# Loading and spreading V of the last batch eight half-slots sooner, and a new order for the first batches, in a windowed attention + MLP kernel

## The chip, the cores and the metric

The kernel runs on one NeuronCore of a Trainium2 chip. Its time is the device time of one execution in microseconds (us). Engines are named as in the profile: PE (TensorE matmul), PEld (its weight loads), DVE (VectorE), ACT (ScalarE), POOL (GpSimd), SP (SyncE). SP only issues DMAs; ACT and POOL issue some as well.

## The reference, cut to what matters

```python
q, k, v: [8 batches, 8 heads, 576 positions, 64]        # float32
scores = q @ k.T / sqrt(64); kept where 0 <= query - key < 64
attn   = softmax(scores);     o = attn @ v               # [8, 8, 576, 64]
x = o.transpose(0, 2, 1, 3).reshape(4608, 512)
h = x @ w_in                                             # [512, 2048]
g = h - tanh(h)
out = g @ w_out                                          # [2048, 512], float32
```

## The kernel before, in words

**Attention.** A batch b has four pairs of heads; a pair is one unit `g = 4*b + pr`, 32 units in all. A unit is worked as follows. Q and K arrive as rows (`load`, `load_all`), are cast to a bfloat16 row tile (`cast`; tiles `qb` and `kb`, three buffers each), and are turned by PE transposes into PSUM, from where ACT or DVE copy them to `qT` and `kT` (`tr`; two buffers each). `scores` makes three groups of three score blocks, with an exponential on ACT behind each group; units below 8 add the mask with a second matmul (`hide`), later units multiply it on DVE (`masking`). `pv` multiplies by V in three groups of three, and `norm` divides on DVE (a reciprocal and two products). Finished heads are turned into `xT`, by PE transposes (`x_tr`) for the first two batches and by DMA transposes (`x_dma`) for the others.

**V.** V of a batch is loaded into one tile `vall` (one buffer: the next load waits until all four casts have read it). Four casts (`cast_v`, one for each pair) bring it to `vb` (one buffer). Nine small DMAs (`keys_v`, 65 KB each) move it to the upper half of `vw[b % 2]`, and a shift (`shift_v`, one DMA of 520 KB on SP, or two DVE copies for the first two batches) fills the lower half. A cast of the next batch into `vb` waits until all nine of these small DMAs have landed. `pv` needs the shift.

**The MLP** is cut into 9 chunks of 512 tokens. For a chunk, `hp_mm` (L304, 16 times) makes h, ACT takes the tanh, `g_sub` (L314, DVE) makes g, and `yp_mm` (L324) multiplies g of 16 slots earlier by w_out; `y_out` copies the result on ACT and stores it from SP.

**The order** is written out by hand. The kernel counts half-slots h; an even h issues `hp_mm`, an odd one `yp_mm`, and then whatever `items[h]` holds. For batches 3 to 7 the items stand in a loop of formulas: for unit g, `a = 8*g - 48 - (0, 2 or 4)` and for its batch `s = 32*b - (0, 2 or 4)`; for the last batch a = 172, 180, 188, 196 and s = 220. The last batch (b = 7) does not use PE transposes for Q and K: it writes the cast rows to DRAM (`bounce`: `qd`, `kd`) and reads them back with a DMA transpose (`tr_dma`), all on SP:

```python
at(a - 12, bounce, g, "q")      # a - 11 for k
at(a - 6, tr_dma, g, "q")       # a - 5 for k
at(s - 54 + j // 2, keys_v, b, j)
at(s - 47, shift_v, b, 0, NJ - 1)
```

`pace(h)` lets POOL wait for the slot's g before it issues a load. The first three batches are in `PLAN`, a table of short codes. The number is a unit (or a batch, or a batch and a part) in base 36, and a last letter names the engine (a ACT, v DVE, p POOL, s SP). The codes of interest are: `q`/`r` load Q/K of a pair; `Q`/`K`/`V` load a whole batch; `a`/`b` cast Q/K; `d` cast V; `k` move keys (`keys_v`); `z` shift; `E`/`F` turn Q/K (`tr`); `R` scores; `P` pv and norm; `X` x_tr; `w`/`o` weights of the two matmuls; `n` the mask; `m`/`i` constants. Key -1 of the table is everything that is issued ahead of the first `hp_mm`. Each engine runs its own instructions in the order of issue, so an order in this table is an order in each engine's queue.

Of the kernel before, what the change touches and what calls it, by code (L numbers as in the profile page):

```python
# [15 lines left out]
def kernel(  # L16
# [12 lines left out]
    NJ = S // 64  # L29
# [307 lines left out]
    def at(h, *fn):  # L337
        items.setdefault(h, []).append(fn)
# [14 lines left out]
    def play(script):  # L353
        for step in script.split():
# [50 lines left out]

    PLAN = {
        -1: """
            r2a q0s v02 v03 v00 v01 a0v r0s d00a d01v d02a m i r1p q3p q1a d03p b0a k01s a1v
            k08s k00s b1p k03p n k02s F0a E0av R01 R02 q2p E1av k07p V1 k06a a3p k04p b2v K1 a2a
            R00 F1v k05s r3a E2aa F2a Q1 w0 R10 z0v d12p R22 d13p R12 P0 R11 E3aa R20 P1 d10p  # L410
            b3a d11p k12s k13p R21 k16p a7p w1 F3a b4a P2 a4p R30 R31 X000v Q2 R32 P3 b7a X001a
            k10s K2 b5p a6p F4a k18s w2 X010v k11s k17s b6p a5p b9p V2 k15a X011v E4vv""",
        0: "b8p",
        10: "R42 F5v k14s E5aa",
        12: "a8v R41 o2 o1 a9p d20p z1v",
        15: "R50 o3 R40 E6av F6v d21p R51 R52 E7aa P4 d22p R62 F7a R61 bAa o0 d23p P5 k25s R60",
        16: "E8aa k23p aAp R70",
        20: "R72 k20s X100v k27s X101a P6",
        23: "F8a R71 F9a k21p k22p aBp R80 P7 E9av k26s bBp k24p R82",
        24: "R81 X111v k28s X110a R91",  # L420
        31: "R90 z2s EAav M8",
        32: "R92",
        35: "FAa",
        36: "RA1 M9",
        41: "P9 RA0 FBa",
        45: "P8 RA2 EBav",
        50: "MA RB2 RB0 PA RB1",
        56: "MB PB",
        58: "Y2",
    }  # L430
    for h, script in PLAN.items():
        at(h, play, script)
# [5 lines left out]
    for g in range(3 * NP, B * NP):  # L438
        b, pr = divmod(g, NP)
        a = 8 * g - 48 - (0, 2, 4)[min(b - 3, 2)]  # L440
        s = 32 * b - (0, 2, 4)[min(b - 3, 2)]
        at(s - 72 + 5 * pr, cast_v, b, pr)
        if b < 7:
            at(a - 7, cast, g, "q")
            at(a, tr, g, "q", 3, nc.scalar, nc.vector)
        else:
            at(a - 14, cast_q, g)
            at(a - 12, bounce, g, "q")
            at(a - 6, tr_dma, g, "q")
        if b < 7:  # L450
            at(a - 5, cast, g, "k")
            at(a + 2, tr, g, "k", 3, nc.scalar)
        else:
            at(a - 13, cast, g, "k")
            at(a - 11, bounce, g, "k")
            at(a - 5, tr_dma, g, "k")
        for i in range(3):
            at(a + 5 + 2 * i, scores, g, i, 4)
        at(a + 11, masking, g)
        for i in range(3):  # L460
            at(a + 13 + i, pv, g, i)
        at(a + 15, norm, g)
        if pr == NP - 1:
            at(a + 16, x_dma, b)
        for j in range(NJ):
            if pr == 0:
                at(s - 54 + j // 2, keys_v, b, j)
        if pr == 0:
            if b < 4:
                at(s - 78, load_v_all, b)  # L470
                at(s - 64, load_all, b, "q")
                at(s - 63, load_all, b, "k")
            else:
                hq, hk = s - (60 if b < 7 else 68), s - (64 if b < 7 else 72)
                for h, f in (s - 78, (load_v_all, b)), (hq, (load_all, b, "q")), (hk, (load_all, b, "k")):
                    at(h, pace, h)
                    at(h, *f)
            at(s - 47, shift_v, b, 0, NJ - 1)

    LAG = 16  # L480
    for h in range(min(items), 2 * (16 * NC + LAG) + 2):
        n = h // 2
        c, m = divmod(n, M)
# [41 lines left out]
```

The softmax here doesn't subtract the row's maximum and nothing guards it: scores larger than these inputs give would overflow.

## Time and profile before

| | |
|---|---|
| median of 4 runs | 353.82 us (352.15 to 355.24) |
| profiled execution: its own time / its span | 352.77 us / 351.1 us |
| PE busy | 315.2 us (90%) |
| DVE, ACT, POOL busy | 198.1, 192.8, 112.0 us |
| first PE instruction | 13.87 us after the span's start |
| first `hp_mm` | 38.90 us |
| last PE work ends, last instruction ends | 347.1 us, 351.1 us |

PE is busy 315.2 us out of 351.1 us, so the idle 35.9 us are what another order could shorten with the same work. They are read by stage: each stretch's length minus its PE busy time. In stretches where PE shows no idle time, what another engine does costs nothing.

### The profile page before, as it was taken

The numbers are of one execution on the slowest core, as the hardware profiler recorded it, in microseconds if no ns is written. First come the engines' busy times: TensorE is split into PE (matmuls) and PEld (weight loads), VectorE is DVE, ScalarE is ACT, GpSimd is POOL, SyncE is SP. The second block draws the span as 40 slices with busy tenths as digits, with TensorE's granted clock in tenths as the row PEclk, the third lists the DMA queues.
The fourth block names the chain that finished last, engine by engine and source line by source line (L and its number), as shares of the span: only waits on it lengthen the run. The fifth ranks groups of instructions, "written<-read, shape, count | busy, mean of one in ns | idle before, by whom it ended". The sixth has DMA issues, their size and how long they took to land.

```text
span 351.1 us, 5740 instructions
## 1 busy us (share of the span) xinstructions
PE 315.2 (90%) x2173; PEld 179.1 (51%) x2173; DVE 198.1 (56%) x314; ACT 192.8 (55%) x347; POOL 112.0 (32%) x160
## 2 busy tenths in 40 slices
PE   0277788899899999999999999997999999999995
PEld 0266456555555555555555555553555444444442
DVE  1336776866776666666767667664656333344400
ACT  1467479865556665666566666553554444444411
POOL 7829633925337424522452262610000000000000
PEclk9999999999999999999999999999999999999999
DMA  8699999969777786877595798559821400010021
GB/s 174 124 157 192 163 191 171 175 132 182 158 157 121 128 124 151 132 146 135 131 132 128 147 158 142 111 141 221 189 74 40 120 32 30 32 59 30 30 90 61
DMA packets 54436, 43.98 MB, mean 125 GB/s; under 512 B 25144, under 2 KB 48248, under 8 KB 54024
## 3 DMA queue, kind: packets, MB, share of 16 engines
q0 software_dynamic: 20512, 18.22, 35.9%
q1 hardware_dynamic: 33128, 24.37, 27.1%
q10 hardware_dynamic: 768, 1.02, 1.0%
q8 instruction: 17, 0.28, 0.3%
q14 instruction: 11, 0.09, 0.1%
HBM read 36.70 MB, written 11.21 MB: 136 GB/s over the span
## 4 chain that ended last, share of the span: by engine, by line
PE 70%; DMA 15%; POOL 5%; DVE 5%; ACT 2%; issue 1%; SPq 0%; ACTq 0%; POOLq 0%; DVEq 0%
PE ps L324 32%; PE ps L304 29%; DMA vw<-vb 5%; DMA vall<-in_v_dram 4%; PE ps L261 4%; DMA kall<-in_k_dram 4%; PE ps L247 3%; PE ps L234 2%; DVE xs L272 2%; DMA vw<-vw 1%; DVE gT L314 1%; POOL vb L84 1%; POOL qb L84 1%; POOL vw L161 1%; DMA kt<-kd 1%
## 5 line engine op out<-in xcount | busy, mean ns | idle before, releaser
L314 DVE TENSOR_TENSOR gT<-ps,th 128x512 bf16<-128x512 f32 x144 | 99.3, 691 | 94.5 <-ACT th L308 92.1
L304 PE MATMUL ps<-xT,wi 128*128 128x512 bf16 x576 | 147.3, 379 | 1.7 <-DVE gT L314 1.7
L324 PE MATMUL ps<-w_out_sb,gT 128*128 128x512 bf16 x576 | 145.2, 379 | 0.2 <-ACT ysb L329 0.2
L308 ACT ACTIVATE th<-ps 128x512 f32<-128x512 f32 x144 | 85.9, 598 | 79.4 <-PE ps L304 79.1
L304 PEld LDWEIGHTS <-wi 128*128 128x128 bf16 x576 | 61.0, 113 | 47.5 <-issue 3.1
L324 PEld LDWEIGHTS <-gT 128*128 128x128 bf16 x576 | 54.1, 98 | 55.8 <-issue 0.5
L251 ACT ACTIVATE pt<-ps 128x384 bf16<-128x384 f32 x96 | 46.9, 490 | 44.5 <-PE ps L247 37.6
L272 DVE TENSOR_TENSOR xs<-ps,rc 64x576 bf16<-64x576 f32 x64 | 48.3, 755 | 1.5
L84 POOL COPY vb<-vall 72x1024 bf16<-72x1024 bf16 x29 | 30.7, 1074 | 52.3 <-DMA vall<-in_v_dram 38.8
L247 PE MATMUL ps<-qt,kt 128*128 128x128 bf16 x288 | 36.8, 227 | 7.7 <-ACT pt L251 3.8
L261 PE MATMUL ps<-vw,pt 128*128 128x130 bf16 x288 | 29.7, 226 | 4.4 <-DMA vw<-vw 1.5
L261 PEld LDWEIGHTS <-pt 128*128 128x128 bf16 x288 | 22.6, 101 | 20.9 <-issue 3.9
L247 PEld LDWEIGHTS <-kt 128*128 128x128 bf16 x288 | 24.5, 102 | 11.4 <-ACT kt L82 1.9
L329 ACT ACTIVATE ysb<-ps 128x512 f32<-128x512 f32 x36 | 21.5, 597 | 16.0 <-PE ps L324 16.0
L84 DVE COPY qt<-ps 64x576 bf16<-64x576 bf16 x24 | 18.2, 759 | 18.7 <-ACT qt L82 18.7
L84 POOL COPY kb<-kall 96x768 bf16<-96x768 bf16 x26 | 21.6, 832 | 13.4 <-DMA kall<-in_k_dram 13.1
L84 POOL COPY qb<-qall 96x768 bf16<-96x768 bf16 x24 | 20.0, 832 | 16.2 <-PE ps L304 6.8
L82 ACT ACTIVATE qt<-ps 64x576 bf16<-64x576 bf16 x32 | 20.4, 636 | 1.2 <-PE ps L234 0.9
L82 ACT ACTIVATE kt<-ps 128x576 bf16<-128x576 bf16 x25 | 16.2, 648 | 4.4 <-PE ps L234 4.2
L255 DVE TENSOR_TENSOR pt<-pt,ps 128x1152 bf16<-128x1152 bf16 x24 | 17.9, 744 | 0.0
L234 PE MATMUL ps<-ident,kb 96*128 96x96 bf16 x168 | 12.6, 214 | 2.0 <-ACT xT L82 0.9
L234 PEld LDWEIGHTS <-kb 96*128 96x128 bf16 x168 | 10.5, 103 | 6.9 <-issue 2.4
(52 smaller groups left out, 123.8 us busy)
## 6 DMA issues: line engine op xcount, KB each, us to landing
out_dram<-ysb SPq DMA_DIRECT2D x36, 256.0 KB
vall<-in_v_dram POOLq DMA_DIRECT2D x7, 576.0 KB, 9.6
kall<-in_k_dram POOLq DMA_DIRECT2D x7, 576.0 KB, 9.2
qall<-in_q_dram POOLq DMA_DIRECT2D x7, 576.0 KB, 8.2
vw<-vb SPq DMA_DIRECT2D x61, 65.0 KB
vw<-vw SPq DMA_DIRECT2D x6, 520.0 KB
w_out_sb<-in_moe_w_out_dram POOLq DMA_DIRECT2D x4, 512.0 KB, 8.6
qd<-qz SPq DMA_DIRECT2D x4, 288.0 KB
```

Of the source, the lines that this page charges most:

```text
L82: nc.scalar.activation(o, i, ACT.Copy)
L84: eng.tensor_copy(o, i)
L234: nc.tensor.transpose(tp[:, e, :], src[:, e, :], ident[:P, :P])
L247: nc.tensor.matmul(sp[:, i, :], kT[g % NR][:, 64 * j:64 * j + 128], qT[g % NR][:, :, 64 * j:64 * j + 64], start=True, stop=g >= 2 * NP)
L251: nc.scalar.activation(PT[g % NPT][:, 3 * grp:3 * grp + 3, :], sp, ACT.Exp, scale=scale)
L261: nc.tensor.matmul(ps[:, 5 + grp, 130 * i:130 * i + 130], PT[g % NPT][:, j, :], vw[b % 2][:, j, 2 * pr:2 * pr + 2, :], start=True, stop=True)
L272: nc.vector.tensor_tensor(xo[r, :, :, pr, :], ov[r, :, :, h, 0:D], rc[r].to_broadcast([64, 3, 3, 64]), ALU.mult)
L304: nc.tensor.matmul(hp, w_in_tile(ki, m), chunk_tile(c)[:, :, ki % 2, 64 * (ki // 2):64 * (ki // 2) + 64], start=(ki == 0), stop=(ki == 3))
L308: nc.scalar.activation(th, hp, ACT.Tanh)
L314: nc.vector.tensor_tensor(gT[c][:, m, :], hp, th, ALU.subtract)
L324: nc.tensor.matmul(yp, gT[c][:, m, s * 128:(s + 1) * 128], w_out_sb[:, m, :], start=(m == 0), stop=(m == M - 1))
L329: nc.scalar.activation(ysb, ps[:, yp_bank(c, s), :], ACT.Copy)
```

## The change

Two parts. **V of the last batch:** a new `sv = s - 8` for b = 7 (212 in place of 220) replaces s in the half-slots of its load and pacing (h = 134, was 142), its four casts (140, 145, 150, 155; were 148, 153, 158, 163), its nine key moves (158 to 162; were 166 to 170) and its shift (165; was 173). Q and K of that batch stay where they were, and so do all bounces and DMA transposes. **The first batches:** the table `PLAN` is written anew. The PE work is the same (4348 PE instructions in both programs); the order and the engine of some copies, key moves and first loads differ.

```diff
-        at(s - 72 + 5 * pr, cast_v, b, pr)
+        sv = s if b < 7 else s - 8
+        at(sv - 72 + 5 * pr, cast_v, b, pr)
...
-                at(s - 54 + j // 2, keys_v, b, j)
+                at(sv - 54 + j // 2, keys_v, b, j)
...
-                for h, f in (s - 78, (load_v_all, b)), (hq, (load_all, b, "q")), (hk, (load_all, b, "k")):
+                for h, f in (sv - 78, (load_v_all, b)), (hq, (load_all, b, "q")), (hk, (load_all, b, "k")):
...
-            at(s - 47, shift_v, b, 0, NJ - 1)
+            at(sv - 47, shift_v, b, 0, NJ - 1)
```

```diff
     PLAN = {
         -1: """
-            r2a q0s v02 v03 v00 v01 a0v r0s d00a d01v d02a m i r1p q3p q1a d03p b0a k01s a1v
-            k08s k00s b1p k03p n k02s F0a E0av R01 R02 q2p E1av k07p V1 k06a a3p k04p b2v K1 a2a
-            R00 F1v k05s r3a E2aa F2a Q1 w0 R10 z0v d12p R22 d13p R12 P0 R11 E3aa R20 P1 d10p
-            b3a d11p k12s k13p R21 k16p a7p w1 F3a b4a P2 a4p R30 R31 X000v Q2 R32 P3 b7a X001a
-            k10s K2 b5p a6p F4a k18s w2 X010v k11s k17s b6p a5p b9p V2 k15a X011v E4vv""",
-        0: "b8p",
-        10: "R42 F5v k14s E5aa",
-        12: "a8v R41 o2 o1 a9p d20p z1v",
-        15: "R50 o3 R40 E6av F6v d21p R51 R52 E7aa P4 d22p R62 F7a R61 bAa o0 d23p P5 k25s R60",
-        16: "E8aa k23p aAp R70",
-        20: "R72 k20s X100v k27s X101a P6",
-        23: "F8a R71 F9a k21p k22p aBp R80 P7 E9av k26s bBp k24p R82",
-        24: "R81 X111v k28s X110a R91",
-        31: "R90 z2s EAav M8",
+            v00 v03 v02 q0s v01 r1p d00a r0s i q1s m d02a d03p b0a b1p r2s a0v d01v k08s F0v
+            k00s E0av k02a k01s q3p k03a a1a E1av q2p n V1 a3p b2p k06a k05s k07p R02 R01 k04p K1
+            r3a F1v a2a d11p R00 R12 Q1 z0v E2av d12a R10 P0 R11 F2a E3va R22 d10v R21 w0 P1
+            d13v b3p w1 R20 F3a P2 a7p k16s b4p k18s R30 X000v k17s R32 k10s a4p K2 k13s a5p R31
+            k14s k11s k12p P3 b7p a6p X001a Q2 k15s b5a w2 b6p X010v X011v b8p E4aa""",
+        0: "F4a",
+        10: "b9p R42",
+        12: "V2 F5v o2 R41 o0 z1v",
+        15: """
+            E5aa o1 R40 a8v R51 d20p F6v E6av a9p R50 d22p R52 d23p E7aa P4 o3 d21p R62 F7a R61
+            k26p P5 k27s bAa R60""",
+        16: "E8aa aAp R70",
+        20: "R72 X101a X100v P6",
+        23: "F8a k25s k20s k28s R71 F9a k23s P7 R82 k22s k24s k21p z2s aBp R81 E9av R80",
+        24: "X111v R91",
+        25: "X110v",
+        31: "bBp FAa R90",
...
```

## The prediction

> **What bounds the kernel now.** First the busy rows by slice, on the page:
>
> ```profile
> PE   0277788899899999999999999997999999999995
> DMA  8699999969777786877595798559821400010021
> ```
>
> PE is the bound from slice 8 (about 70 us) on; ahead of it PE is starved while the DMA engines are full. Idle by stretch, from the windows of busy time: 13.87 us before the first PE instruction, 10.98 from there to 60 us, 2.99 from 60 to 100, 4.0 from 100 to 300, of which 2.56 lie between 230 and 250, and 4 at the end (the last copy and store). Only these 35.9 us can move. The waits of PE from 225 to 260 us name the 2.56:
>
> ```profile
> PE ps L247 <- DMA kt<-kd: 1.4, 1, 1.4
> PE ps L261 <- DMA vw<-vw: 1.2, 1, 1.2
> ```
>
> SP's own timeline shows why those two DMAs come late (start, length with the wait in it):
>
> ```profile
> 229.91 2.38 SPq L161 DMA_DIRECT2D vw<-vb  x2
> ...
> 232.83 0.87 SPq L161 DMA_DIRECT2D vw<-vb  x1
> 235.16 0.52 SPq L169 DMA_DIRECT2D vw<-vw  x1
> 235.79 2.76 SPq L137 DMA_TRANSPOSE qt<-qd  x1
> 238.59 1.26 SPq L140 DMA_TRANSPOSE kt<-kd  x1
> ```
>
> The shift (L169) waits for the last key move, and the transposes of unit 29 stand behind it. The front's binding chain is in the chain of waits, in order of time:
>
> ```profile
> 35.73 13.55 DMA kall<-in_k_dram
> ...
> 50.20 9.57 DMA vall<-in_v_dram
> ...
> 70.08 6.73 DMA vw<-vb
> ...
> 76.99 4.22 DMA vw<-vw
> 81.21 0.05 issue
> 81.26 0.63 PE ps L261 x8
> ```
>
> K of batch 2 lands, POOL casts a piece, V of batch 2 (V2) is issued, its casts and key moves follow, then the shift; unit 9's pv waits 0.31 us for it. So at 81.26 PE and the V2 chain are nearly level: PE gaining time before that point keeps it only if the V2 chain gains too.
>
> **Part 1, V of the last batch (h = 134 to 165).** No instruction is added or removed; nine key moves, the shift, four casts and a load move ahead.
>
> *On SP.* The key moves go ahead of the bounces and transposes of units 28 and 29. Four are issued from about 209.6 (the last cast follows unit 26's cast), at some 0.65 each. The bounces of unit 28 wait, as before, for Q of this batch, which lands at 217.0 (`qz` cast 216.98): 218.3 and 219.6. The last key move is issued at 221.3, about 2 us to land (before, 232.83 + 0.87 to the shift at 235.16), shift at 223.4, landing 4.2 later (76.99's row) at 227.6; pv of unit 28 reads it at 238.46. Transposes of unit 28 follow at 223.9 and 225.2 (before 221.01, 223.78), landing near 228.5; scores of unit 28 want them at 230.71: 2 us of cover. Unit 29: transposes issued by 233.2 in place of 239.85; wanted at 240.1. Both stalls go: **-2.56**.
>
> *What is late next:* unit 30. Its transposes ended at 247.90 on SP and its scores began at 249.53 with a gap of only 0.09; they stood behind two xT transposes (241.51, 3.08). That group is issued some 2.5 us sooner too, as far as PE is. I charge 0.1.
>
> *On POOL.* The new load stands after unit 24's cast (188.27), so at 189.1. The first V cast now stands ahead of unit 25's Q cast (before at 189.81) and waits for the load. PE turns unit 25 at 200.69. Landing times of V loads here: 7.9 (195.7's) to 11.1 (15.0's), median 9.6. With 9.1 (160.5's, the one whose place in its batch is like this one's): 198.2, + 1.05 V cast + 0.84 Q cast = 200.1, in time; at 11.1 a stall of 1.4. The overlap with batch 6's key moves (to 191.9) and shift (193.64) speaks for 9 to 10. I charge 0.2. Part 1: **-2.3**, between -2.6 and -1.0.
>
> [...] The row first: at 230 to 240 us the DMA share is 0.70, not full, and the delay is SP's in-order wait between the last key move (232.83) and the shift (235.16), not bytes. [...]
>
> **Part 2, the new table.** Same PE work; I walk the new order with durations of the rows (a cast 0.83 or 1.05, DMA issue 0.65 to 0.85, six transposes 0.66 and 0.42, score triple 0.8 cold and 0.5 warm; matmuls start 0.107 apart until 33.16 and 0.055 after, and I keep that moment).
>
> - *Start.* PE waited for the mask (POOL, 13.87). Now K and Q of unit 0 stand ahead of the mask: V casts on ACT from about 7.9, kb at 11.0, PE at 11.1: -2.8 at the first instruction. It hides nothing yet: pv of unit 0 needs key moves behind V of batch 1 in POOL's DMA ring.
> - *pv of unit 0.* V1 is issued at 13.5 (was 15.02) and took 11.1; with the key moves behind it landing at 24.5 (was 26.36), pv ends at 25.9 (was 27.78): -1.9.
> - *First `hp_mm`.* Less was done ahead of pv (R22 and F2 move behind it), DVE has 0.76 + 2 x 0.43 more between the norms, and each pv waits for a norm (0.22 + 1.52): P1 29.0, P2 32.0, P3 34.6, `hp_mm` at 38.3 (was 38.90): -0.6. Q1 and w0 are issued at 25.6 and 26.4 (were 17.98 and 18.76) because POOL's V1 cast now stands ahead of them; in the old order POOL stood still behind them instead. They land near 33 and 35.5: w0 has some 3 us of cover.
> - *h = 0 to 15.* F4 is now behind the first `hp_mm` and E5 in h = 15 with both copies on ACT (1.29) in front of the exponentials on which the next scores wait: R40 48.5, R51 50.9, F6 51.2, R50 51.9, R52 53.1, P4 53.7, P5 56.2, ninth `hp_mm` 57.1 (was 56.50): **+0.6**. The lead is gone.
> - *V2 chain.* Its load now stands behind unit 9's K cast, whose buffer F6 frees: cast 51.5, V2 at 52.4 (was 50.20). Then: landing 8.8 (between 7.9 and 9.57, as w2 is further on), 61.2; casts, one Q cast and weight load to V3's issue 6.95 (was 6.81), 68.2; the one key move behind V3 in the ring lands with it, 9.5 + 0.4, 78.1 (was 76.81); shift 0.2 + 4.2; pv of unit 9 at **82.5** (was 81.26). PE arrives at 81.3 to 81.4, so the chain decides: **+1.25**. Later gates have slack: batch 3's shift is wanted only at 105.7, nine us after it landed.
>
> [...]
>
> **Sum.** -2.3 + 1.25 = -1.0 us: 352.77 - 1.0 = 351.8 for the profiled execution, which lies 1.05 below the median; from 353.82, **352.8 us**.
>
> **Rivals.**
>
> 1. *The gate doesn't bind* (0.25). V2 and V3 land in 7.9 us, as one load did, and the lead at pv of unit 0 (-1.9) survives h = 15. Against it: ACT's two copies there. Then part 2 gives -2 and the whole -4.3: 349.5.
> 2. *V2 comes later, slower* (0.17). Q2 and w2 (2.1 MB read) now wait for E4's buffer and go out at 39.3 and 40.1 (were 34.93 and 38.04). w2 took 17.0 us, and V2 landed 4.7 behind it. If the ring is emptied late, w2 at 60 (the ninth `hp_mm` wants it at 57.1) and V2 at 64.7: gate 86.0, +4.7 - 2.3: 356.2. It decides once V2 lands after 62.3, where part 1 is used up. For it: at 20 to 60 us the DMA share is about 1; against it: fewer bytes are left in front of w2.
> 3. *Part 1 doesn't do what it says* (0.08): unit 25's cast or unit 30's transposes stall by what unit 29 gains. Then only +1.25 stays: 355.1.
>
> The forecast has 0.50. **Range** 349.0 to 357.0: the first reaches to rival 1, the second past rival 2. About 1% (3.5 us) is what a measurement here can tell from no change. Faster by more: most of rival 1, 0.22; slower: much of rival 2 and tails, 0.18; within 1%: 0.60.
>
> **What would show it.** First PE work near 11 us; pv of unit 0 ending near 26; first `hp_mm` at 38.3; ninth near 57; V2 issued near 52.4; pv of unit 9 waiting for `vw<-vw` by about 1 us, near 82.5; no PE wait for `vw<-vw` or `kt<-kd` at 225 to 260; at most a few tenths on unit 25's transpose near 202. A V2 landing before 60 or after 63, or a ninth `hp_mm` off by over 2 us, makes it wrong.

## The result, and the profile after

The changed kernel takes 355.77 us, the median of 32 runs (353.84 to 359.10), against 353.87 us of the kernel before beside it; the ratio is 1.0075 (95% interval 1.0056 to 1.0095). So it is **slower by 0.75%**, a small change, but clear of the noise. Its profiled execution took 355.78 us with a span of 354.1 us, 3.0 us more than the span before. PE is busy as long as before (315.1 us). The forecast was a gain of 1.0 us.

The rows by slice, of the changed kernel:

```profile
PE   0258777898899999999999989999999999999995
...
PEclk9999899999999999999999999999999999999999
DMA  8699996976986959786597689488701410010011
```

Read against the rows before, slices counted from 0: PE's 7 at slice 27 has become a 9, which is part 1's gain. The 8 at slice 23 is new. In the front, slices 2 to 6, three of PE's digits are lower, one is equal and one is higher. PEclk has an 8 in slice 4, where the page of before has 9 throughout. (The 9s ahead of it do not mean full speed, see below at the clock.)

**The tail.** From 225 to 260 us the list of PE's waits has no row at all: both stalls, 1.4 and 1.2 us, are gone. PE is busy for all of these 35.00 us; before it was for 32.44. SP's timeline of that stretch, changed kernel (start, length with the wait in it):

```profile
228.41 0.52 SPq L169 DMA_DIRECT2D vw<-vw  x1
229.04 2.77 SPq L137 DMA_TRANSPOSE qt<-qd  x1
231.85 1.25 SPq L140 DMA_TRANSPOSE kt<-kd  x1
...
236.78 1.23 SPq L137 DMA_TRANSPOSE qt<-qd  x1
238.10 1.21 SPq L140 DMA_TRANSPOSE kt<-kd  x1
```

The shift goes out at 228.41 in place of 235.16, although PE is six microseconds later than before by then. It now stands in front of the transposes of unit 28 (229.04, 231.85), and those of unit 29 (236.78, 238.10) no longer stand behind it. But from 110 to 225 us a wait is new (PE's waits, changed kernel):

```profile
PE ps L234 <- POOL qb L84: 1.4, 1, 1.4
```

That is unit 25: its Q cast stands on POOL behind the first V cast, and that one waits for the load.

**The front.** PE's timeline (start, length, and in brackets the idle time before it and its releaser), of the kernel before:

```profile
27.19 0.59 PE L261 MATMUL ps<-vw,pt 128*128 128x130 bf16 x4 [0.52 <-DVE vw L167]
28.21 0.69 PE L234 MATMUL ps<-ident,qb 96*128 96x96 bf16 x6
29.65 1.14 PE L261 MATMUL ps<-vw,pt 128*128 128x130 bf16 x9
...
37.00 0.41 PE L234 MATMUL ps<-ident,kb 96*128 96x96 bf16 x6 [0.85 <-ACT xT L82]
```

And of the changed kernel:

```profile
27.08 0.59 PE L261 MATMUL ps<-vw,pt 128*128 128x130 bf16 x4 [0.52 <-DVE vw L167]
...
30.79 1.18 PE L261 MATMUL ps<-vw,pt 128*128 128x130 bf16 x9
...
40.27 1.91 PE L304 MATMUL ps<-xT,wi 128*128 128x512 bf16 x4
41.97 0.69 PE L234 MATMUL ps<-ident,kb 96*128 96x96 bf16 x6
```

pv of unit 0 ends at 27.67, as late as before (27.78). pv of unit 1 starts 1.14 us later than before (29.65), the first `hp_mm` 1.37 later (38.90), the ninth at 60.00 (56.50). The four matmuls at 40.27 take 1.70 us to the next instruction; four of them take 0.86 later (81.04 to 81.90). The busy windows show why (columns: PE, PEld, DVE, ACT, POOL, granted clock, DMA share, GB/s):

```profile
39.00:40.00 1.00, 0.77 (x12) 0.64 (x13) 0.65 (x2) 0.00 (x0) 0.69 (x1) 0.79 0.95 184
40.00:41.00 1.00, 1.00 (x8) 0.56 (x7) 0.26 (x2) 0.45 (x1) 0.04 (x1) 0.50 1.03 132
...
43.00:44.00 1.00, 1.00 (x6) 0.48 (x5) 0.54 (x1) 0.61 (x2) 1.00 (x2) 1.00 1.03 207
```

The granted clock is at half (0.50) from 39.6 to 43.0, in the middle of the first matmuls of the MLP.

pv of unit 0 waits for the last key moves of batch 0. POOL's timeline of the changed kernel shows why these are late:

```profile
11.81 0.82 POOL L84 COPY kb<-kall 96x768 bf16<-96x768 bf16 x1 [2.02 <-DMA kall<-in_k_dram]
...
15.21 0.84 POOL L151 DMA_DIRECT2D vall<-in_v_dram  x1 [0.39 <-issue]
...
18.78 1.18 POOL L161 DMA_DIRECT2D vw<-vb  x2
```

POOL waits for K of unit 1, issues V of batch 1 (V1) at 15.21 (before 15.02), and reaches the two key moves behind it only at 18.78.

**The V2 chain.** POOL's timeline, changed kernel: the load of V2 stands behind a K cast that waits for PE (and so does an earlier K cast, at 50.20).

```profile
54.55 0.82 POOL L84 COPY kb<-kall 96x768 bf16<-96x768 bf16 x1 [3.52 <-PE ps L234]
55.32 0.86 POOL L151 DMA_DIRECT2D vall<-in_v_dram  x1
```

It goes out at 55.32 (before 50.20). The chain of waits ends that way at 86.2, where unit 9's pv has waited 1.5 us:

```profile
73.41 7.92 DMA vw<-vb
81.58 4.62 DMA vw<-vw
```

So by marks the changed kernel is late by 1.4 at the first `hp_mm`, by 3.5 at the ninth and by 5.0 at pv of unit 9 (81.26 before). Then follow 4.7 ahead of unit 25, 6.3 behind it and 3.3 behind the tail, by the starts of the same matmuls in both; the spans differ by 3.0.

### The profile page after: what moved, and what is told of

It reads as the page before. It is cut to its first block, busy times and chain, and to the rows that moved or that the text cites. A ratio compares the mean times of both kernels' runs of the same rounds, so it can differ in the third digit from the quotient of the medians.

```text
span 354.1 us, 5753 instructions
## 1 busy us (share of the span) xinstructions
PE 315.1 (89%) x2173; PEld 179.6 (51%) x2173; DVE 198.8 (56%) x315; ACT 193.0 (55%) x346; POOL 108.7 (31%) x156
## 3 DMA queue, kind: packets, MB, share of 16 engines
q1 hardware_dynamic: 33760, 25.16, 27.3%
## 4 chain that ended last, share of the span: by engine, by line
PE 74%; DMA 11%; DVE 5%; ACT 4%; POOL 2%; issue 2%; SPq 1%; POOLq 0%; ACTq 0%; DVEq 0%
PE ps L324 31%; PE ps L304 30%; DMA vw<-vb 6%; PE ps L261 5%; PE ps L247 4%; PE ps L234 3%; DVE xs L272 2%; DMA kall<-in_k_dram 2%; DVE gT L314 1%; DMA vw<-vw 1%; DMA qall<-in_q_dram 1%; ACT qt L82 1%; ACT pt L251 1%; ACT th L308 1%; POOL vall L146 1%
## 5 line engine op out<-in xcount | busy, mean ns | idle before, releaser
L251 ACT ACTIVATE pt<-ps 128x384 bf16<-128x384 f32 x96 | 46.8, 490 | 37.8 <-PE ps L247 33.1
L84 POOL COPY vb<-vall 72x1024 bf16<-72x1024 bf16 x26 | 27.8, 1077 | 57.6 <-DMA vall<-in_v_dram 42.4
L329 ACT ACTIVATE ysb<-ps 128x512 f32<-128x512 f32 x36 | 21.5, 596 | 16.0 <-PE ps L324 15.7
L84 POOL COPY qb<-qall 96x768 bf16<-96x768 bf16 x24 | 19.9, 830 | 25.8 <-DMA qall<-in_q_dram 24.6
L84 DVE COPY qt<-ps 64x576 bf16<-64x576 bf16 x23 | 17.5, 760 | 17.7 <-ACT qt L82 17.6
L234 PE MATMUL ps<-ident,kb 96*128 96x96 bf16 x168 | 12.9, 218 | 12.8 <-ACT kb L82 12.1
```

Source lines behind the costliest of these rows:

```text
L84: eng.tensor_copy(o, i)
L234: nc.tensor.transpose(tp[:, e, :], src[:, e, :], ident[:P, :P])
L251: nc.scalar.activation(PT[g % NPT][:, 3 * grp:3 * grp + 3, :], sp, ACT.Exp, scale=scale)
L329: nc.scalar.activation(ysb, ps[:, yp_bank(c, s), :], ACT.Copy)
```

## The experiments

Ratios are against the kernel before, run beside each; spans are those of the profiled execution. The theories: **A**, the new table costs the time (through waits that the runs below name one by one); **B**, V sooner costs it; **T**, PE's clock in the front is a part of its own.

### Which part

Part 1 alone, in the kernel before:

```diff
+        sv = s if b < 7 else s - 8       # s -> sv in load, casts, key moves, shift
```

> The kernel before with part 1 alone (the table of the first batches stays old). Theory A (the table costs the time): both stalls of 225 to 260 us go (-2.56), unit 25's transposes wait about 1.4 us for a Q cast that stands behind the first V cast (+1.4): span 350.0, about 1.1 us below before. Rival B (V sooner costs it): the load of V among batch 6's key moves takes back more than it gives: span 351 to 353, no gain or a loss.

Measured: ratio 0.9960 (0.9925 to 0.9994), span 350.2. No PE wait from 225 to 260 us. POOL's timeline of it at unit 25:

```profile
189.22 0.82 POOL L151 DMA_DIRECT2D vall<-in_v_dram  x1
...
200.98 1.05 POOL L84 COPY vb<-vall 72x1024 bf16<-72x1024 bf16 x1 [10.11 <-DMA vall<-in_v_dram]
201.97 0.82 POOL L84 COPY qb<-qall 96x768 bf16<-96x768 bf16 x1
```

The load was cast 11.8 us after its issue, and PE waited 2.0 us for the Q cast behind it.

The new table alone:

```diff
-        sv = s if b < 7 else s - 8
+        sv = s
```

> The changed kernel with the V of the last batch at its old half-slots (the new table alone). Theory A: ninth hp_mm near 60.0 (before 56.50), pv of unit 9 near 86.2, both stalls of 225 to 260 us back: span 355.2, 4 us above before. Rival B: the new table costs at most the forecast 1.25, span near 352.4, and the rest comes from part 1.

Measured: ratio 1.0115 (1.0069 to 1.0161), span 356.1. The PE waits from 225 us on are those of before again, to the tenth, and unit 25 does not wait. The two ratios multiply to 1.0075, the ratio of both parts together. Theory A holds and B falls: **part 1 gives 0.4%, the new table costs 1.15%**.

### Part 1 without its own stall

```diff
-        at(sv - 72 + 5 * pr, cast_v, b, pr)                       # v_qfirst
+        at(sv - (72 if b < 7 else 70) + 5 * pr, cast_v, b, pr)
```
```diff
-        sv = s if b < 7 else s - 8                                # v_four
+        sv = s if b < 7 else s - 4
```

> Part 1 alone with its four V casts two half-slots later (142, 147, 152, 157), so that unit 25's Q cast stands ahead of the first V cast on POOL; load, key moves and shift as in part 1. Theory A (the order on POOL makes the stall): unit 25's wait of 1.4 us goes, the gain of 2.56 stays: span 348.6, 2.5 us below before. Rival C (the landing of V is late in itself and the key moves of batch 6 share its DMA engines): the Q cast goes but another wait comes, span 350 or more.

> Part 1 alone by four half-slots in place of eight (load 138, casts 144 to 159, key moves from 162, shift 169). Theory A: the first V cast comes behind unit 25's Q cast, so no wait there; key moves and shift stand ahead of the transposes of unit 29 by enough: both stalls gone or nearly, span 348.6 to 349.2. Rival C: unit 28's transposes, issued at the same half-slots as the last key moves (166 and 167), wait for those, and a stall of 1 us or more stays: span 350 or more.

Measured: 0.9942 (0.9907 to 0.9976), span 348.4; and 0.9943 (0.9906 to 0.9981), span 347.3. In both the wait at unit 25 is gone, though V lands no sooner (the first cast of it is at 201.29 and 202.07). POOL of v_qfirst:

```profile
191.84 0.82 POOL L84 COPY qb<-qall 96x768 bf16<-96x768 bf16 x1
201.29 1.05 POOL L84 COPY vb<-vall 72x1024 bf16<-72x1024 bf16 x1 [8.63 <-DMA vall<-in_v_dram]
```

The Q cast runs nine microseconds ahead of the V cast in place of behind it. So the stall came from the order on POOL and not from bytes (rival C falls). With four half-slots only 0.2 us of wait is left in the tail, so the transposes of unit 28 do not suffer. Neither ratio can be told from that of part 1 alone; the waits in the traces are what separates them.

### Which stretch of the new table

The old table ahead of the first `hp_mm`, the new one behind it, with part 1:

```diff
     PLAN = {
-        -1: """ (new) """, 0: "F4a", 10: "b9p R42", 12: "V2 F5v o2 R41 o0 z1v",
+        -1: """ (old, with b9p V2 and F4a) """, 0: "b8p", 10: "R42 k14s", 12: "F5v o2 R41 o0 z1v",
         15: """ (new)
```

> Part 1 with the old table ahead of the first hp_mm and the new table from half-slot 0 on (V2 stays where the old table had it, and so do unit 8's and 9's K casts and F4). Theory B (the loss is made ahead of the first hp_mm): first hp_mm 38.9, ninth 57.2 (E5's copies in half-slot 15 cost 0.7), span 350.2 to 351, ratio near 0.998. Rival I (the new order after slot 0 costs most): ninth 58.5 or later, span 352.5 or more.

Measured: 0.9945 (0.9914 to 0.9975), span 350.5; first `hp_mm` 38.22, ninth 57.90. This is as fast as part 1 alone. So **the whole loss is made by what the new table issues ahead of the first `hp_mm`, or has pushed from there into the first slots** (V2, unit 9's K cast, F4). Theory B of this run holds; the order from slot 15 on costs nothing that can be measured.

### Undoing the named waits

Three edits of the changed kernel, one by one and together:

```diff
-  ... R12 Q1 z0v E2av d12a R10 P0 R11 F2a E3va R22 d10v R21 w0 P1       # a_hoist
+  ... R12 Q1 E2aa R10 R11 F2a R22 R21 E3aa z0v P0 d12a d10v w0 P1
```
```diff
-  b6p X010v X011v b8p E4aa""", 0: "F4a", 10: "b9p R42", ... 15: "E5aa o1 R40   # a_f4e5
+  b6p F4a X010v X011v b8p E4aa""", 10: "b9p R42 E5aa", ... 15: "o1 R40
```
```diff
-  b8p E4aa""", ... 12: "V2 F5v                                          # a_v2
+  V2 b8p E4aa""", ... 12: "F5v
```

> The changed kernel, with the scores of units 1 and 2 and the turning of units 2 and 3 put back in front of pv of unit 0 (ACT does both halves of E2 and E3; ACT's cast of V behind them). Theory A1 (2.8 us of cold PE work stand between pv of unit 0 and pv of unit 1 where PE used to idle for V): pv of unit 0 unchanged at 26 to 27, pv of unit 1 starts near 29.6 (changed kernel 30.79), first hp_mm 39.0 (40.27), span 352.8, about 1.3 us less. Rival D (the norms on DVE set this stretch alone): pv of unit 1 earlier, first hp_mm as late as 40.2, span 354.

> The changed kernel with two copies put back: F4 in front of the last xT transposes (out of half-slot 0) and E5 at half-slot 10 (out of 15). Theory A2 (F4 lies on PE's path in slot 0; ACT's two copies of E5 stand in front of the exponentials): first hp_mm unchanged at 40.3, PE's wait of 1.79 for pt in half-slot 15 falls below 1, ninth hp_mm 58.7 (60.00), and 57.8 if the clock stays up; span 352.8. Rival E (the wait only moves to the next exponential): ninth hp_mm within 0.5 of 60.0, span 353.6 to 354.1.

> The changed kernel with the load of V2 issued ahead of unit 8's K cast, so that it waits for no K buffer. Theory A3: V2 issued near 44 (55.32), its casts no longer late, V3 issued 4 to 5 us sooner; PE's wait of 1.5 us at pv of unit 9 goes, but PE itself comes late, so no more than that: span 352.6. Rival F (the gate at unit 9 holds the whole loss): span 350 to 351. Rival G (V2 among Q2 and w2 delays w2, which the ninth hp_mm wants): ninth hp_mm later than 60.5, span 354 or more.

> The changed kernel with the three edits above together. Theory A: they are the whole loss of the new table and add up: first hp_mm 39, ninth 57.5, no wait at pv of unit 9, span 350 to 350.5, like the old table with part 1. Rival H (a further cost in the new table, the start or the colder clock): span 351.5 or more.

| | ratio (interval) | span | pv of unit 0, last group | pv of unit 1 | first, ninth `hp_mm` | clock at half up to, and again |
|---|---|---|---|---|---|---|
| before | 1 | 351.1 | 27.19 | 29.65 | 38.90, 56.50 | 31.9 |
| changed | 1.0075 (1.0056 to 1.0095) | 354.1 | 27.08 | 30.79 | 40.27, 60.00 | 32.8; 39.6 to 43.0 |
| a_hoist | 1.0119 (1.0079 to 1.0159) | 356.2 | 28.49 | 30.95 | 41.89, 61.77 | 21.9; 25.3 to 38.9, 42.4 to 45.8 |
| a_f4e5 | 1.0065 (1.0038 to 1.0092) | 353.9 | 28.31 | 32.02 | 41.32, 59.34 | 21.1; 24.6 to 34.8, 68.9 to 72.4 |
| a_v2 | 1.0067 (1.0029 to 1.0104) | 353.0 | 27.35 | 31.06 | 40.63, 60.61 | 21.6; 25.0 to 31.9, 38.7 to 42.1, 55.8 to 59.2 |
| a_all | 1.0053 (1.0016 to 1.0090) | 351.7 | 27.17 | 29.63 | 40.57, 59.16 | 19.0; 25.8 to 36.1, 39.5 to 42.9 |

Each edit did to its own wait what it should. In a_hoist pv of unit 1 follows 2.46 us behind pv of unit 0, in place of 3.71. In a_f4e5 the wait of 1.79 us for `pt` in half-slot 15 is 0.22. In a_v2 V2 goes out at 44.39, and the wait at pv of unit 9 is gone. Yet the time hardly followed: a_hoist is no faster at all, and none of the four can be told from the changed kernel by its interval. The spans expected (352.8, 352.8, 352.6, and 350 to 350.5 for all) were all too low; a_v2 came nearest, and its ninth `hp_mm` (60.61) has rival G's sign, though PE waits for no weights there. In what was expected of a_all, rival H's number was right: something else remains. The last column points to it.

**How that column is read.** The page and the windows give the clock as 1.00 from the start up to the first change on record, and that is not the clock. In the kernel before, six transposes take 0.69 us at 28.21, as long as six of them take at 41.97 in the changed kernel, where 0.50 is on record; at 37.00 they take 0.41. In the trace, the starts inside the group of six at 31.60 go from 0.080 us apart to 0.042 at 31.9, and there the clock's first record, a 1.00, begins. In a_all_warm (below) six transposes take 0.69 us at 18.78 and 0.42 at 20.86, with 1.00 on the page at both. So these profiled executions begin at half clock, and the first number of the column is the end of that. What sets the changed kernel and the four others apart from the kernel before is half clock after 32 us.

### The clock

Two kernels with filler matmuls whose result nobody reads, in PE's waits of the front; the second also has the three edits above:

```diff
+            elif what == "f":      # fBnn: nn matmuls of 128 columns into bank B
+                for _ in range(int(step[2:])):
+                    nc.tensor.matmul(ps[:, int(step[1]), 0:128], ident,
+                                     hide.rearrange("p h t -> p (h t)"), start=True, stop=True)
-  R10 P0 R11 ... X001a Q2            # a_warm
+  R10 f748 P0 R11 ... X001a f026 Q2
-  F2a R22 R21 E3aa z0v P0 d12a d10v w0 P1 ... b6p F4a                    # a_all_warm
+  F2a f718 R22 R21 E3aa z0v f720 P0 d12a d10v w0 f020 P1 ... b6p f012 F4a
```

> The changed kernel with filler matmuls that nobody reads (128 columns each, into a PSUM bank free at that time): 48 in front of pv of unit 0, where PE waits 4.2 us for V, and 26 in front of the last xT transposes, where it waits 1.6 us. Theory T (PE's clock, which falls to half where PE was idle for about half of a stretch of 3.4 us, makes the new table's front slower than its waits do): no granted clock below 1.00 between 30 and 45 us, first hp_mm at 38.6 to 39.2 (40.27), ninth at 57.2 to 58 (60.00), span 351.3 to 352. Rival A (the waits alone): the clock stays up, but first and ninth hp_mm move by less than 0.7, span 353.4 or more.

> The kernel with the three undone edits (a_all) and fillers in its four waits of the front (18, 20, 20 and 12). Theory T: no clock below 1.00 from 27 us on, third pv at 32.2 (32.63), first hp_mm 38.2 (40.57), ninth 56.2 (59.16), span 349 (351.7): with the edits undone the clock was what was left. Rival A: span 351 to 352, so the rest lies after the ninth hp_mm.

a_all_warm: ratio 0.9993 (0.9954 to 1.0032), span 351.7, first `hp_mm` 39.35, ninth 57.38. The windows of a_all and then of a_all_warm (columns as above):

```profile
30.00:35.00 5.00, 4.25 (x43) 4.14 (x41) 3.96 (x8) 1.62 (x3) 1.68 (x3) 0.50 1.19 181
35.00:40.00 5.00, 3.33 (x40) 2.77 (x38) 3.16 (x6) 3.00 (x6) 4.64 (x7) 0.84 1.12 199
```

```profile
30.00:35.00 5.00, 3.33 (x52) 2.98 (x52) 4.24 (x9) 1.92 (x4) 2.34 (x3) 1.00 1.01 134
35.00:40.00 5.00, 3.73 (x51) 2.90 (x50) 3.73 (x8) 3.05 (x7) 4.26 (x6) 1.00 1.21 212
```

From its first rise at 20.8 us on, the clock stays at 1.00, and from pv of unit 0 to the ninth `hp_mm` 29.07 us pass in place of 31.99: 2.9 us less, in a profile in which the last key move of batch 0 landed 1.1 us later. The ratio moves the same way, with intervals that just overlap. But the span is the one of a_all, 351.7, as rival A had it. PE's timeline shows where the 1.8 us gained by the ninth `hp_mm` went:

```profile
83.88 0.63 PE L261 MATMUL ps<-vw,pt 128*128 128x130 bf16 x8 [1.76 <-DMA vw<-vw]
```

pv of unit 9 waits again for V2's shift, which it did not in a_all. So here the gate of the prediction is seen at work: PE gained ahead of it, the V2 chain did not, and the whole gain was taken back.

a_warm: ratio 1.0073 (1.0038 to 1.0108), span 352.6; first `hp_mm` 38.74, as theory T had it, but the ninth at 59.27. Here the clock fell elsewhere, from 28.2 to 31.6 and from 52.1 to 58.9, where PE waits for the exponentials behind E5's copies. Fillers in two waits alone do not keep it up, so this run neither supports nor refutes T.

The old table shows what one fall costs. v_only, v_four and v_qfirst have the same program in the front, but in the profile of v_qfirst the clock was at half from 37.8 to 41.2. The first `hp_mm` of v_four, and then of v_qfirst:

```profile
38.16 2.00 PE L304 MATMUL ps<-xT,wi 128*128 128x512 bf16 x8
```

```profile
38.60 4.34 PE L304 MATMUL ps<-xT,wi 128*128 128x512 bf16 x12
```

From the first `hp_mm` to the ninth 18.7 us pass in v_qfirst, and 17.6 in v_four and v_only. In b_f4 and b_both (below) F4 stands in the same place; with a fall that stretch takes 19.1 us, without one 17.7. So one fall at this place costs 1.1 to 1.4 us, and it is not peculiar to the new table.

Every execution also lists its mean granted clock (0.983 on average in the changed kernel, about 0.99 in the kernel before). No share can be read from these means, as they too count the time up to the first record as full: 0.995 of 354.1 us leaves room for some 3.5 us at half, the fall at 39.6 alone. The changed kernel and plan_only have the same front. Their clocks rose first at 32.8 and at 19.7, and fell at the first `hp_mm` in both; their means are 0.995 and 0.981, and their ninth `hp_mm` came at 60.00 and 60.25. **So theory T holds in the profiles in which the clock falls; how much of the 0.75% it makes is not shown.**

### Is one choice of the new table enough?

The kernel before with one choice of the new table each, and with both:

```diff
-  E2aa F2a Q1 w0 R10 z0v d12p R22 d13p R12 P0 R11 E3aa R20 P1          # b_late
+  E2aa Q1 w0 R10 z0v d12p d13p R12 P0 R11 F2a E3aa R22 R20 P1
-  b5p a6p F4a k18s ... 0: "b8p"                                        # b_f4
+  b5p a6p k18s ... 0: "F4a b8p"
```

> The kernel before with one choice of the new table: K of unit 2 turned and its third scores made behind pv of unit 0 (before: in front of it, where PE waits for V). Theory A1: pv of unit 1 starts 3.7 us behind the last group of pv of unit 0 (before 2.46), first hp_mm 40.1 (38.90), span 352.3, ratio 1.0035. Rival D (V2's chain and the norms swallow it): first hp_mm within 0.4 of 38.9, ratio within 0.001 of 1.

> The kernel before with one other choice of the new table: K of unit 4 turned in half-slot 0 in place of in front of the last xT transposes, so that PE waits some 1.6 us there. Theory T: first hp_mm as before (38.9); granted clock at half for 3.4 us from 38 to 43 in more than half of the executions; hp_mm 2 starts 0.5 later, and 1.3 to 1.8 later where the clock falls; ratio 1.002 to 1.005. Rival A (no clock in it): ratio 1.001 or less.

> The kernel before with both choices. Theory A1 and T: they add, first hp_mm 40.1, ninth 58.5 to 59.5, ratio 1.006 to 1.008. Rival L (something else in the new front, such as its start or V of batch 1, makes most of the loss): ratio 1.004 or less.

Measured: 1.0002 (0.9963 to 1.0042), 1.0004 (0.9970 to 1.0039) and 1.0037 (0.9995 to 1.0079). In b_late the 3.71 us between pv of unit 0 (26.47) and of unit 1 (30.18) are as expected (2.46 before), yet the first `hp_mm` came at 39.12: V's last key move landed sooner here, and the next pv followed after 2.7 in place of 3.0 us. At pv of unit 9 PE waits 1.8 us for V2's shift (before 0.31). So rival D had both numbers. In b_f4 the clock fell from 37.7 to 41.1 in the profile, and from the first `hp_mm` (38.12) to the ninth (57.26) 19.1 us passed in place of 17.6. In the profile of b_both it did not fall, and the same stretch took 17.7 us. **Neither choice by itself makes a loss that can be measured**, so for b_late and b_f4 the expected ratios were too high, and the rivals' numbers were right (for b_f4 the number alone, as the clock did fall in its profile). Both together, by the point value, are a third of the table's 1.15%, with an interval that reaches below 1, and rival L of b_both had the number.

### What remained

In a_all_warm the last key move of batch 0 went out behind V1 and two casts on POOL. Put ahead of V1:

```diff
-  q2p n V1 a3p b2p k06a k05s k07p R02 R01 k04p K1
+  q2p k07p k04p n V1 a3p b2p k06a k05s R02 R01 K1
```

> a_all_warm with the two key moves of batch 0 that POOL issues put ahead of the load of V1 (before, behind V1 and two casts: issued at 19.4 to 20.6, landed at 27.5). Theory N (these two make the rest of the loss): they land by 23, DVE's shift is free by 24, pv of unit 0 ends by 27 (28.9), first hp_mm 37.9 (39.35), span 350.3 or less, ratio 0.995. Rival M (bytes or a later stage take it back): ratio 0.998 or more.

Measured: 0.9974 (0.9943 to 1.0006), span 349.8. DVE's copy of the shift, which waits for the last key move:

```profile
24.53 0.70 DVE L167 COPY vw<-vw 64x2080 bf16<-64x2080 bf16 x1 [3.65 <-DMA vw<-vb]
```

In a_all_warm that copy starts at 27.56, in the changed kernel at 26.33. pv of unit 0 starts at 25.20 without a break, the ninth `hp_mm` is at 56.66, and pv of unit 9 waits for nothing. The span is as theory N had it; the ratio lies between its number and rival M's. With five corrections (the three edits, the fillers and the key moves) the changed kernel has come down from 1.0075 to 0.9974, and these two intervals are apart. It lies 0.14% from the old table with the same part 1 (v_only, 0.9960), and 0.3% from `of` (0.9945), both within the intervals. The key moves alone, without the other four, were not tried in the changed kernel.

### Versions that go further

Part 1 by four half-slots on the old table, with POOL's last key moves of batch 0 ahead of V1 and V2 ahead of unit 9's K cast (v_best); the same with ACT's key move on SP (v_best2); and that with two pieces of `w_in` loaded sooner (v_best3):

```diff
-  k07p V1 k06a a3p k04p b2v K1 ... a5p b9p V2 k15a
+  k07p k04p V1 k06a a3p b2v K1 ... a5p V2 b9p k15a        # v_best; k06s in v_best2
-  Q1 w0 R10 ... a7p w1 F3a ... F4a k18s w2 X010v
+  Q1 w0 w1 R10 ... a7p w2 F3a ... F4a k18s X010v          # v_best3, with v_best2's edits
```

> The old table with V of the last batch four half-slots sooner, the last two POOL-issued key moves of batch 0 ahead of the load of V1, and V2 ahead of unit 9's K cast. Theory J (pv of unit 0 waits for a key move that stands behind V1 in POOL's DMA ring, and unit 9 for a V2 that stands behind a K cast): last key move lands before 24, pv of unit 0 ends near 25.9 (27.78), first hp_mm 37.4 (38.90), V2 issued near 40 (50.20), no wait at pv of unit 9, span 345.8, ratio near 0.990. Rival K (another key move lands as late, or the clock falls in the waits that open): pv of unit 0 as before, span 347.3 and more, ratio 0.994.

> The old table with V of the last batch four half-slots sooner, V2 ahead of unit 9's K cast, and all the key moves of batch 0 issued ahead of or beside V1: the one that ACT issued at 18.3 (landing 25.9) now goes out on SP near 15. Theory J: last key move lands by 23, DVE's shift no longer the wait, pv of unit 0 at 25.7 without a break (26.78), first hp_mm 37.6 (38.50), span 347.2, ratio 0.991. Rival M (bytes, not the issue, set the landing: K1, Q1 and V1 fill the DMA engines): lands at 25 to 26 again, ratio 0.9935.

> v_best2 with the second and third piece of w_in loaded one place sooner (the second beside the first, the third where the second stood). Theory O (their landing made the waits of 1.70 and 1.05 us on the fifth and ninth hp_mm): both waits go, ninth hp_mm near 54 (56.45), span 345.5, ratio 0.987. Rival P (other loads now come late, V of batch 1 or K of batch 2, and are waited for): ninth hp_mm 56 or later, ratio 0.992 or more.

v_best: 0.9935 (0.9907 to 0.9964); pv of unit 0 ends at 27.37, only 0.4 sooner than before. Its chain of waits names the key move that ACT issues behind its exponentials (rival K):

```profile
18.26 7.65 DMA vw<-vb
```

v_best2: **0.9923 (0.9886 to 0.9959)**, median 350.69 us, faster than the kernel before and the changed one, but not to be told from v_four (0.9943), which has the same part 1 alone. The shift's copy starts at 23.93, pv of unit 0 runs from 24.61 with no break, the first `hp_mm` stands at 36.45 (38.90). Then PE waits for weights, and at the ninth `hp_mm` nothing is left of the 2.45 us (56.45, before 56.50):

```profile
42.65 1.92 PE L304 MATMUL ps<-xT,wi 128*128 128x512 bf16 x8 [1.70 <-DMA wi<-in_moe_w_in_dram]
...
56.45 1.05 PE L304 MATMUL ps<-xT,wi 128*128 128x512 bf16 x4 [1.05 <-DMA wi<-in_moe_w_in_dram]
```

v_best3: 0.9971 (0.9941 to 1.0001), so rival P: both waits go, and Q of batch 2, loaded behind the weights, takes their place. One line of PE's timeline, one of the chain:

```profile
55.30 0.64 PE L234 MATMUL ps<-ident,qb 96*128 96x96 bf16 x6 [4.75 <-DVE qt L84]
```

```profile
35.60 15.71 DMA qall<-in_q_dram
```

Q2 lands 15.7 us after its issue; DVE stands at a cast for it, and PE behind DVE for 4.75 us. From 34.2 to 51.3 us the DMA share is 1.09 to 1.48 in this profile, so the reading is that a load moved forward took its time from the next; no run separates this from the order in POOL's queue.

## Why the prediction was wrong

**Part 1, the tail: right.** The idle 2.56 us between 225 and 260 are gone to the last hundredth, and unit 30 did not wait (0.1 was charged). By the starts of the matmuls the tail gained 3.0.

**Part 1, unit 25: right mechanism, wrong size.** The step named the V cast ahead of the Q cast, and "at 11.1 a stall of 1.4", and then took a landing of 9.1 and charged 0.2. Here V was cast 10.6 us after its issue in the changed kernel and 11.8 in part 1 alone; the waits are 1.4 and 2.0. The landings known were 7.9 to 11.1 with a median of 9.6, and the one below the median was chosen although the load was being moved into a neighbour's key moves. Part 1 gave 0.4% in place of 0.65%.

**Part 2, start: the step that failed first.** PE began at 12.12 (11.1 predicted), which mattered little. But "V1 is issued at 13.5" was 15.21: POOL first waits for K of unit 1, which landed 7.5 us after its issue, and only then reaches V1; the two key moves behind V1 go out at 18.78, and PE has them at 26.29. So "pv ends at 25.9" was 27.67, and of the lead of 1.9 only 0.1 was there. From there the walk was right within 0.2: P1, P2, P3 and the first `hp_mm` were put 3.1, 6.1, 8.7 and 12.4 us behind the end of pv of unit 0, and came 3.1, 6.2, 8.7 and 12.6 behind. Of the error of 2.0 at the first `hp_mm` (38.3 against 40.27), 1.8 is that one landing.

The step was also built on half of what pv of unit 0 waits for. It took the key moves behind V1 in POOL's ring for the only late ones. In v_best both of POOL's go ahead of V1 in the old table, and the shift's copy starts at 26.03 in place of 26.44, because a key move that ACT issues at 18.26 lands 7.65 us later. Only with that one on SP as well (v_best2) does the copy start at 23.93. Whether a key move behind V1 is held by V1's place in the ring or by the full DMA engines is not shown: both fit the changed kernel.

**Part 2, the clock: a silent assumption failed.** "And I keep that moment" held the clock up after 33.16 because it did so in the profile of before (where the rise is in fact at 31.9; 33.16 is the first pair of scores behind it). It fell again for 3.4 us at the first `hp_mm`, and the ninth came 0.9 us later, counted from the first, than the walk had it. One fall there costs 1.1 to 1.4 us in other pairs of profiles, so it is enough for the 0.9.

**Part 2, V2: right mechanism, wrong size.** The order of the steps is as told: unit 9's K cast waits for F6, V2 stands behind it. As PE was late, V2 was late too: 55.32 (52.4 predicted), V3 69.86 (68.2), and the last key move and the shift needed 12.8 us from 73.41 on, so pv of unit 9 started at 86.25 (82.5). +1.25 became +5.0 in the profile and +1.15% in the runs. Of the 5.0, only 1.2 is a longer wait at the gate (1.54 against 0.31); the rest is PE's own lateness, 84.49 against 80.73 at the first matmul of that pv. That is why V2's early load alone (a_v2) brought so little.

**The rivals.** Rival 2 ended at 356.2 with the gate at 86.0, and the profile shows 355.78 and 86.25. The number is right, but by luck, as the mechanism is not: w2 did not come late (no PE wait for `wi`); V2 landed at 62.8, just past its point of 62.3, because it was issued late. The forecast, "the chain decides by 1.25", was too cheap, since it took a lead from an unchecked start into every later step.

**Order and landings.** At the tail the step went by the order on SP and not by bytes, and that was right: the same bytes went through the same queue, and 2.56 us came from the order. For V2 it went by the landings in the profile of before, 7.9 to 9.57 us, and put 8.8; V2 was cast 7.5 us after its issue.

**What stays open.** How the 1.15% divide between the late key moves, the order around pv of unit 0, F4, V2 and the clock is not settled: no single edit moves the ratio beyond its interval, and the clock falls at other places each time. Shown is only that, put right together (with fillers for the clock), they undo the loss within the intervals, and that it is made by what belongs ahead of the first `hp_mm`.

## What to carry to other kernels

Before an early lead is carried through a chain of steps, check its first landing: which instructions of the issuing engine wait ahead of that DMA, and for what. A cast must not stand behind another cast whose load may be late if PE wants the first one sooner; moving it two half-slots removed a wait of 2 us. Where PE has many short waits, count them per 3.4 us as well as in sum: here the granted clock fell to 0.50 behind 19 stretches of that length in which PE was busy 0.55 of the time or less, and one such fall at the first `hp_mm` cost 1.1 to 1.4 us. And a gain ahead of a gate counts only once the gate has moved as well: in a_all_warm 1.8 us were gained ahead of V2's shift and lost there.

## What the runs showed of the hardware

**The changes of the granted clock were 3.4 us apart, or a whole multiple of it.** Twelve profiles were read in steps of 0.05 us up to 66 us (the changed kernel, plan_only, v_qfirst, `of`, a_hoist, a_f4e5, a_v2, a_all, a_warm, b_f4, a_all_keys and v_best3). From the first fall on, the times between two changes in them are 3.4, 6.8, 10.2, 13.7, 20.5 and 27.3 us; in the changed kernel 6.8 us pass from the first rise to the fall. Ahead of the first rise six transposes take as long as at 0.50 (0.69 us at 28.21 in the kernel before and at 20.36 in the changed kernel), which the record does not show.

Cut into stretches of 3.41 us, with the changes at their ends, these twelve profiles have 19 falls up to 66 us, each behind a stretch in which PE was busy 0.00 to 0.55 of the time. Of the other 66 stretches at 1.00, two were busy 0.48 (a_hoist, from 52.60) and 0.50 (plan_only, from 50.40), and 64 were busy 0.59 or more; no fall followed them. The 19 rises came behind stretches busy 0.83 to 1.00, and the first rises of the kernel before and of the changed kernel behind 0.92 and 0.94. The clock stayed at half behind a stretch busy 0.83 in a_warm (from 52.09), and behind one busy 0.82 ahead of the first rise of the changed kernel (from 19.10). So in these profiles half idle was mostly enough for a fall, and a rise came only behind a stretch nearly full. No long wait stood ahead of the fall at 39.6: PE is busy 1.61 of the 3.41 us in front of it, and its longest wait there is 1.6 us.

The changes were not tied to the kernel's start. With the same front, the first rise is at 32.8 us in the changed kernel and at 19.7 in plan_only, where the matmuls from 19.02 to the first group of pv take 1.63 us (2.37 in the changed kernel). Of v_only, v_four and v_qfirst only the last one's clock fell in the front, behind a stretch busy 0.55.

**Fillers held the clock up in one of three kernels.** Fillers in four waits kept it at 1.00 from its first rise to the end of PE's work in the profiled execution of a_all_warm. In a_all_keys, with the same fillers, it was at 0.50 from 32.4 to 35.8, and fillers in two waits (a_warm) let it fall twice.
